# Last pass of a two-layer attention and MLP training step: weights turned from four neighbouring rows, sums in natural order, w2's gradient units moved out of w1's phase

## The chip, the cores and the metric

The kernel runs on one core of one Trainium2 chip. Its time is device microseconds of one execution. The kernel before took a median of 1111.3 us in 3 runs (1110.21 to 1113.48).

## The reference

The reference is the output and all gradients of two identical layers on two tokens (B = 2, one query position, D = 1024). The two layers share their weights, and each is attention over a cache and then an MLP:

```
def A(x): q = x @ wq; p = softmax(q . k_cache / sqrt(128)); o = p . v_cache; return o @ wo
          # 32 query heads, 4 cached heads of 16384 positions x 128, wq [1024, 4096], wo [4096, 1024]
def B(x): return gelu(layernorm(x) @ w1 + b1) @ w2 + b2        # w1 [1024, 3584], w2 [3584, 1024]
x = A_x
for layer in (0, 1):
    x = x + A(layernorm(x))
    x = x + B(layernorm(x))
out_0 = x
out_1..out_9 = gradients of x, k_cache, v_cache, wq, wo, w1, b1, w2, b2, by vjp with grad_out
```

All tensors are bfloat16. The gradients of the caches (out_2 and out_3) are 67 MB, those of the matrices 31 MB.

## The kernel before

The kernel makes four passes over the cache: attention forward for layer 0 and for layer 1 (`attn_fwd`), then backward for layer 1 and for layer 0 (`attn_bwd`). Each goes over 8 pairs of token and cached head, in 16 steps each, a step being 1024 cached positions; each 1 MB chunk of K or V serves four steps. Between the passes lie the MLP phases. The backward pass of layer 0 is the last pass, and it also forms and stores all the large gradients.

**The order of the work.** The program is first written down as a list of operations (`emit`), and each names the chunks (1 MB buffers) that it uses. `Program.run` then walks the list and issues on SP's queue the load of the next chunk as soon as a buffer fits it; an issued load waits, in that queue, until the earlier users of its buffer are done. `slots` at the end of the kernel says which piece of memory is a buffer of which kind, from which operation to which: "load" for inputs, "half" (512 KB) and "full" (1 MB) as staging for outputs. Sixteen tiles `slot_tiles` start as "load" buffers; three of them become "half" ones (`HALF_AT`, two of them just before w1's last phase) and four "full" ones (`FULL_AT`: steps 4, 8, 12, 16 of the last pass). Two more areas become staging later on (`marks["done", ...]`). `keep` lets a chunk of the same key stay in its buffer from one use to the next where there is room.

**A product with a turned weight.** The backward pass multiplies by transposed weights. In the last pass a chunk of four blocks of 128 weight rows is loaded by `ld_rows`, "(j p) n -> p j n": partition p gets rows p, 128 + p, 256 + p and 384 + p of the four. `turn_rows` (two instructions a chunk, line 433) transposes it on VectorE in blocks of 32 x 32 elements of 4 bytes, each a pair of bfloat16, into a second buffer; each block is written as 32 adjacent elements ("p (w j m)"). `turned_products` (line 483) then uses 128 x 128 pieces of it as TensorE weights against `vb`, a copy of the vector spread block-diagonally over four groups of 32 partitions by `spread` (lines 502 and 503). The sums come out in PSUM in an order that depends on the transpose: the quarter j of 32 rows of every group is in partitions 32 j to 32 j + 31, the group in the column. `unquad` brings them into natural order: one copy from PSUM to the tile `uq` (line 513) and 16 copies of 32 partitions each (lines 521 on VectorE, 523 on ScalarE, 525 on POOL, dealt out by its string `on`).

The chunks turned so in the last pass are

- w1, eight chunks of 896 columns (`ws1c`, turned by `t1`, multiplied by `p1`), before the pass, for the gradient of the MLP's input (`dm_0`, `mlp_in_bwd(0, ...)`);
- wo, two chunks for each of three cached heads (`wo_bwd_ops` through `turned_pair`), for the gradient of the heads' outputs, which `do_of` takes up;
- wq, two chunks for each of three cached heads (`wq_bwd_ops`), summed in PSUM and taken out once by `dn_kept` into `dnq`.

**w1's phase.** After the pass of layer 1: four transposes of w1 `t1[0:4]`, then the 28 products with w2 (`here_products`, line 461, sums `dhps0`) with `t1[4:9]` between them, then `dh0_` (line 1500) and its spread, then `t1[9:]`, and then the eight products `p1`. After each of these the kernel emits one or two pieces of `first`, the gradient of w2 (out_8): `y_rows` (line 1266) and `x_rows` (lines 1281 and 1286) build the two factors, each unit is one TensorE product of 512 columns (line 1303) and one eviction on ScalarE (line 272) or VectorE (line 275), and every fourth unit issues a store of 512 KB on POOL (line 1329). Nine pieces go between and behind the products, six after the sums of the layer norm (`g1p[0]`, line 645 on), the rest (`rest_h`) into the background list `bg`, from which the last pass takes `max(1.3, len(bg) / (120 - s))` pieces at each step s from 5 on. The sums end in `gA_all`, with which the last pass begins (`wo_prods0`).

**The end.** The last step is 133. The outputs of the caches are formed in units of 512 columns (line 1248); a chunk of 1 MB is stored by line 1253 after eight of them. The last pair's K chunks are worked off two steps at a time in steps 126 to 133, and what is left of the outputs, the last wq products and out_1 follow.

Of the kernel before, what the change touches and what calls it, by code (L numbers as in the profile page):

```python
# [10 lines left out]
I32 = mybir.dt.int32  # L11
# [10 lines left out]
SPARE = (3, 4)  # L22
HALF_AT = (-1, -1, 18)
FULL_AT = (4, 8, 12, 16)
N_HALF = len(HALF_AT)
N_FULL = len(FULL_AT)
SKEW = 2
# [151 lines left out]
def kernel(  # L179
# [98 lines left out]
    def dve(us):  # L278
        load_of("dve", us)
# [92 lines left out]
    def ld_rows(nm, W, j0, rb, c0, n):  # L372
# [2 lines left out]
            ap[:, 0:rb * n].rearrange("p (j n) -> p j n", j=rb),  # L375
            W[j0 * 128:(j0 + rb) * 128, c0:c0 + n].rearrange("(j p) n -> p j n", p=128)), (nm, j0, c0))

    def ld_wq(k):
        return [ld_rows("wq", A_wq, 4 * i, 4, k * 1024, 1024) for i in range(2)]

    def ld_wo(k):
        return [ld_rows("wo", A_wo, 8 * k + 4 * i, 4, 0, 1024) for i in range(2)]
# [41 lines left out]
            emit(*pend.pop(0))  # L424


    def turn_rows(c, t, ncol=1024):

        nw = ncol // 128

        def f(h):
            def fn():
                V.transpose(out=t.ap[:, h * nw * 256:(h + 1) * nw * 256].bitcast(I32).rearrange(  # L433
                    "p (w j m) -> p w j m", j=4, m=32), in_=c.ap[:, 0:4 * ncol].bitcast(I32).rearrange(
                        "p (j n) -> p j n", j=4)[:, :, h * nw * 32:(h + 1) * nw * 32].rearrange(
                            "p j (w m) -> p w j m", m=32))
                dve(1.23)
            return fn

        return [(f(h), [c, t]) for h in range(2)]  # L440
# [34 lines left out]
    def turned_products(ps, t, w0, nw, vb, first, last, parts=1):  # L475

        def f(k):
            def fn():
                tv = t.ap[:, 0:nw * 256].rearrange("p (w x e) -> p w x e", x=128, e=2)
                for w in range(k * nw // parts, (k + 1) * nw // parts):  # L480
                    for e in range(2):
                        J = (w0 + w) // 2
                        PE.matmul(ps(), lhsT=tv[:, w, :, e], rhs=vb()[:, 2 * (w % 2) + e, :, 2 * J:2 * J + 2],
                                  start=(first and w == 0 and e == 0), stop=(last and w == nw - 1 and e == 1),
                                  skip_group_check=True)
            return fn

        return [(f(k), [t]) for k in range(parts)]
# [17 lines left out]

        return (lambda: hold["vb"]), fn

    def unquad(dst, src, on="vag"):

        C = src.shape[1]
        q = small.tile([128, 8, 4, 2], F32, name="uq", bufs=1)[:, 0:C]
        V.tensor_copy(out=q, in_=src)
        n = 0
        for a in range(4):
            for j in range(4):
                d, s_ = dst[32 * a:32 * a + 32, :, j], q[32 * j:32 * j + 32, :, a]
                e = on[n % len(on)]
                n += 1
                if e == "v":  # L520
                    V.tensor_copy(out=d, in_=s_)
                elif e == "a":
                    S.copy(out=d, in_=s_)
                else:
                    GP.tensor_copy(out=d, in_=s_)
# [415 lines left out]
    def turned_pair(ws, acc, vb):  # L941

        ts = [P.chunk() for _ in ws]
        res = []
        for i in range(2):
            res += turn_rows(ws[i], ts[i]) + turned_products(lambda i=i: acc[:, i], ts[i], 0, 16, vb, False, True, 2)
        return res

    def wo_bwd_ops(l, k, vb):

        acc = sb[0][:, 64:80].rearrange("p (c a b) -> p c a b", c=2, a=4)

        def fin():
            raw = small.tile([128, 8, 2], F32, name="do_raw")
            unquad(raw[:].rearrange("p (c j) b -> p c j b", j=4), acc)
            V.memset(sb[0][:, 64:80], 0.0)
            dve(1.1)
            do_of(l, k, raw[:])

        return turned_pair(ld_wo(k), acc, vb), (fin, ())  # L960

    def wo_first_ops(l, k, ws=None):

# [35 lines left out]
    def wq_bwd_ops(l, k):  # L999

        acc = sb[0][:, 96:112].rearrange("p (c a b) -> p c a b", c=2, a=4)
        hold = {}

        def sp():
            vb, fn = spread(lambda: dq_all[:, k * R:(k + 1) * R, 2 * l:2 * l + 2], 8, "vg")
            hold["vb"] = vb
            fn()

        return [(sp, ())] + turned_pair(ld_wq(k), acc, lambda: hold["vb"]())

    def wq_last_ops(l, k):

# [7 lines left out]
    def attn_bwd(l, order, gT, wo_first, outputs=None, mark=None, extra=None):  # L1020
# [49 lines left out]
        dnq = wrk.tile([128, DJ, 2], F32, name="dnq")  # L1070

        def dn_kept():
            unquad(dnq[:].rearrange("p (c j) b -> p c j b", j=4),
                   sb[0][:, 96:112].rearrange("p (c a b) -> p c a b", c=2, a=4), "g")

        tail = []
        for i, k in enumerate(kvs):
# [313 lines left out]
    def at_sb0(c0, n):  # L1391
        return sb[0][:, c0:c0 + n]
# [79 lines left out]
    for n, b in enumerate(w2_turns):  # L1472
        extra.setdefault(28 + 3 * n, []).append(b)

    ws1c = [ld_rows("w1q", B_w1, 4 * h, 4, cg * 896, 896) for h in range(2) for cg in range(4)]
    dm_0 = quads(at_sb0(224, 16))
    vh0, spread_h0 = spread(lambda: dh_all[:, :, 0:2], FJ, "vh")
    t1, p1 = [], []
    for n, c in enumerate(ws1c):
        t = P.chunk()  # L1480
        t1 += turn_rows(c, t, 896)
        p1 += turned_products(lambda n=n: dm_0[:, n // 4], t, 14 * (n % 4), 14, vh0, n % 4 == 0, n % 4 == 3)
    for n, b in enumerate(t1[0:2]):
        extra.setdefault(135 + 2 * n, []).append(b)
# [24 lines left out]
        emit(*b)  # L1509
    emit(lambda: load_of("dve", 6.0))  # L1510
    first = [y_rows(gM_all, 0, 8, 0, 0)] + dw_units("h", 0, 0, pieces_rows(out_8, F, D))
    rest_h = first[15:]
    for n, b in enumerate(p1):
        emit(*b)
        for u in first[n + (n > 0):n + 2]:
            emit(*u)
    va0, spread_a0 = spread(lambda: gA_all[:, :, 0:2], DJ, "va")
    g1p = mlp_in_bwd(0, lambda dm: unquad(dm[:].rearrange("p (c j) b -> p c j b", j=4), dm_0), g2, parts=True)
    emit(g1p[0])
    emit(lambda: load_of("dve", 6.0))  # L1520
    for u in first[9:15]:
        emit(*u)
    emit(lambda: saved.__setitem__("g1", g1p[1]()))
    extra = {4: [(spread_a0, ())]}
# [22 lines left out]
    def outputs(s, rest=False):  # L1547
        if rest:
            fin = late.pop(s)
            return fin[0:1], sum([sched.pop(x) for x in sorted(sched)], []), bg + fin[1:]  # L1550
        if s in STAGE:
            mark(s)()
        if s in (68, 78):
            mark("done")(s // 78)
        res = list(sched.pop(s, ()))
        if s in late:
            bg.extend(late.pop(s))
        if s >= 5:
            state["credit"] += max(1.3, len(bg) / (120 - s)) if s < 116 else 3
        while bg and state["credit"] >= 1:  # L1560
            res.append(bg.pop(0))
            state["credit"] -= 1
        state["credit"] = min(state["credit"], 2.0)
        return res
# [2 lines left out]
    attn_bwd(0, down, lambda: saved["g1"], (va0, wo_prods0), outputs=outputs, extra=extra)  # L1567
    slots = []
    for i, t in enumerate(slot_tiles):
        until = marks[(HALF_AT + FULL_AT)[i], 0] if i < N_HALF + N_FULL else None  # L1570
        slots.append((t[:], "load", 0, until))
        if i < N_HALF:
            slots += [(t[:, j * 2048:(j + 1) * 2048], "half", until, None) for j in range(2)]
        elif i < N_HALF + N_FULL:
            slots.append((t[:], "full", until, None))
    slots += [(Et[1][:, i * CH:(i + 1) * CH], "load", 0, marks["e1", i]) for i in range(2)]
    slots += [(D1t[:, i * CH:(i + 1) * CH], "load", 0, marks["d1", 1 - i]) for i in range(2)]
# [37 lines left out]
```

## Time and profile before

| | |
|---|---|
| time, median of 3 runs | 1111.3 us (1110.21 to 1113.48) |
| time of the profiled execution | 1111.95 us |
| its span | 1110.2 us |
| TensorE, VectorE, ScalarE, POOL busy | 820.1, 762.1, 493.0, 182.5 us |
| mean granted TensorE clock | 0.722 |
| moved by DMA | 450.03 MB, mean 405 GB/s |
| loads (SP's queue), stores (POOL's queue) | 349.22 MB, 98.62 MB |

The span is the stretch between the first and the last record of the profile; the time includes 1.75 us around it. Busy times are sums over the whole span, through stages with different limits, so they don't say what bounds any of them. The mean rate is to be held against the rate in the slices where the DMA engines are full.

### The profile page before, as it was taken

To read this page: it belongs to the slowest core of one execution; us is meant where nothing else is said; L and a number is where in the kernel's file an instruction comes from. 1 tells how busy PE (TensorE), PEld (TensorE's weight loads), DVE (VectorE), ACT (ScalarE), POOL (GpSimd) and SP (SyncE) were. 2 spreads that over 40 slices of the span, in tenths; PEclk is the share of its full clock that TensorE was granted. 3 is DMA by queue.
4 is the path that set the end of the run, shared out by engine and by line. 5 is a ranking of instruction groups with operands and counts; after the bars stand their busy time and mean duration, and the time that the engine had idled before them with its cause. 6 is when DMAs were issued, how large, how long until landed. Compare 5 with 4: busy or idle time off the path is not lost. (4 is left out here: it accounts for less than half of the span.)

```text
span 1110.2 us, 34189 instructions
## 1 busy us (share of the span) xinstructions
PE 820.1 (74%) x14689; PEld 610.7 (55%) x14689; DVE 762.1 (69%) x1474; ACT 493.0 (44%) x1133; POOL 182.5 (16%) x577
## 2 busy tenths in 40 slices
PE   5665666457887647888778678978867986798886
PEld 4554565456777537887767564444433443344453
DVE  5864675069888637665646466978877895698874
ACT  0422223002233222245444327767766784577873
POOL 1000000001000000111111102324232332333331
PEclk9755555555555556568878658989997997699996
DMA  9999999999999998999999989999999999999994
GB/s 379 420 422 422 422 425 420 394 402 404 415 422 422 422 420 352 411 418 418 418 423 421 416 321 414 348 405 423 419 420 427 422 419 422 419 409 420 412 422 204
DMA packets 97448, 450.03 MB, mean 405 GB/s; under 512 B 7528, under 2 KB 11638, under 8 KB 58512
## 3 DMA queue, kind: packets, MB, share of 16 engines
q1 hardware_dynamic: 79504, 349.22, 77.2%
q0 software_dynamic: 17792, 98.62, 21.5%
q8 instruction: 115, 1.88, 0.6%
q14 instruction: 37, 0.30, 0.1%
HBM read 349.20 MB, written 98.62 MB: 403 GB/s over the span
## 5 line engine op out<-in xcount | busy, mean ns | idle before, releaser
L533 DVE STREAM_TRANSPOSE kT<-slot 128x512 int32<-128x512 int32 x420 | 283.4, 694 | 109.6 <-PE sc L546 86.6
L546 PE MATMUL sc<-qbd,kT 128*128 128x32 bf16 x4096 | 262.5, 222 | 11.9 <-DVE kT L533 10.4
L546 PEld LDWEIGHTS <-kT 128*128 128x128 bf16 x4096 | 209.2, 115 | 64.2 <-issue 33.3
L571 PEld LDWEIGHTS <-slot 128*128 128x128 bf16 x3520 | 144.5, 103 | 108.5 <-issue 48.1
L571 PE MATMUL sb<-xt,slot 128*128 128x8 bf16 x3520 | 161.2, 177 | 49.0 <-DMA slot<-in_A_v_cache_dram 24.4
L272 ACT CAST slot<-sc 128x512 bf16<-128x512 f32 x293 | 167.0, 593 | 64.4 <-PE sc L1303 38.9
L1248 PE MATMUL sc<-slot,late 128*128 128x512 bf16 x349 | 133.2, 404 | 17.4 <-DVE slot L275 5.4
L275 DVE CAST slot<-sc 128x512 bf16<-128x512 f32 x171 | 114.5, 678 | 30.6 <-PE sc L1248 16.2
L756 ACT ACTIVATE e<-sc 128x512 bf16<-128x512 f32 x32 | 19.0, 597 | 235.3 <-DVE sc L753 168.4
L272 ACT CAST slot<-sb 128x512 bf16<-128x512 f32 x139 | 82.5, 593 | 36.3 <-PE sb L1303 18.4
L451 ACT COPY slot<-tp 128x512 int32<-128x512 int32 x88 | 50.2, 586 | 108.6 <-PE tp L448 108.3
L448 PE MATMUL tp<-ident,slot 128*128 128x128 bf16 x768 | 72.0, 256 | 13.1 <-DMA slot<-in_A_wq_dram 7.1
L1248 PEld LDWEIGHTS <-late 128*128 128x128 bf16 x512 | 44.8, 99 | 59.5 <-issue 46.9
L581 ACT COPY xt<-e 32x128 int32<-32x128 int32 x256 | 75.6, 295 | 3.9
L1248 PE MATMUL sb<-slot,late 128*128 128x512 bf16 x163 | 66.6, 409 | 12.7 <-DVE slot L275 7.8
L1303 PE MATMUL sc<-slot,late 128*128 128x512 bf16 x160 | 64.4, 424 | 11.2 <-DVE e L275 6.2
L448 PEld LDWEIGHTS <-slot 128*128 128x128 bf16 x768 | 58.3, 117 | 15.7 <-DMA slot<-in_A_wq_dram 7.7
L433 DVE STREAM_TRANSPOSE slot<-slot 128x1024 int32<-128x1024 int32 (+1 forms) x48 | 55.3, 1178 | 16.0 <-DMA slot<-in_A_wo_dram 8.4
L275 DVE CAST slot<-sb 128x512 bf16<-128x512 f32 x81 | 54.9, 678 | 11.6 <-PE sb L1248 4.0
L638 POOL TENSOR_TENSOR m_rstd<-ln_vpe,neghalf 128x2 f32<-128x2 f32 x2 | 1.4, 716 | 349.8 <-DVE ln_vpe L636 349.8
L581 POOL COPY xt<-late 32x64 int32<-32x64 int32 x240 | 55.2, 230 | 13.0 <-DVE late L1042 1.9
L1253 POOL DMA_DIRECT2D out_dram<-slot x57 | 31.1, 546 | 157.1 <-ACT slot L272 115.2
(303 smaller groups left out, 1105.0 us busy)
## 6 DMA issues: line engine op xcount, KB each, us to landing
slot<-in_A_k_cache_dram SPq DMA_DIRECT2D x105, 1024.0 KB, 17.3
slot<-in_A_v_cache_dram SPq DMA_DIRECT2D x98, 1024.0 KB, 17.5
out_dram<-slot POOLq DMA_DIRECT2D x57, 1024.0 KB, 14.1
slot<-in_A_wq_dram SPq DMA_DIRECT2D x25, 1024.0 KB, 16.0
slot<-in_A_wo_dram SPq DMA_DIRECT2D x25, 1024.0 KB, 20.2
out_dram<-slot POOLq DMA_DIRECT2D x43, 512.0 KB, 14.2
slot<-in_B_w_dram SPq DMA_DIRECT2D x23, 896.0 KB, 15.5
slot<-in_B_w_dram SPq DMA_DIRECT2D x12, 1024.0 KB, 13.0
```

What stands on the lines that cost most here:

```text
L272: S.copy(out=dst, in_=src)
L275: V.tensor_copy(out=dst, in_=src)
L433: V.transpose(out=t.ap[:, h * nw * 256:(h + 1) * nw * 256].bitcast(I32).rearrange("p (w j m) -> p w j m", j=4, m=32), in_=c.ap[:, 0:4 * nc ...
L448: PE.transpose(tp[:, j * 128:(j + 1) * 128], c.ap[:, off + j * 128:off + (j + 1) * 128], ident[:])
L451: S.copy(out=d.bitcast(I32), in_=tp.bitcast(I32))
L533: V.transpose(out=kT[:].bitcast(I32).rearrange("p (w j m) -> p w j m", w=4, j=4), in_=c.ap[:, (i % 4) * 1024:(i % 4 + 1) * 1024].bitcast(I ...
L546: PE.matmul(sc[:, a0:a0 + 4, :, 2 * (i % 4) + q], lhsT=kv[:, 2 * q + w, :, e], rhs=qbd[:, q_at(g), 2 * w + e], start=(w == 0 and e == 0), ...
L571: PE.matmul(acc, lhsT=c.ap[:, n * 128:(n + 1) * 128], rhs=xv[:, i // 4, t // 2, :, 2 * (i % 4) + t % 2], start=(fresh and i == 0 and t == ...
L581: (GP.tensor_copy if on[t % len(on)] == "g" else S.copy)(out=d[32 * t:32 * t + 32, c0:c0 + cn, j, :], in_=s[32 * j:32 * j + 32, c0:c0 + cn ...
L1248: PE.matmul(ps, lhsT=hold["blk"][:, j, :], rhs=flat(qm(w)[:, (u % 2) * 4:(u % 2) * 4 + 4, :]), start=True, stop=True)
L1253: GP.dma_start((dKv if w == 0 else dVv)[g, :, c * 32:(c + 1) * 32, :], stg.ap.rearrange("p (t d) -> p t d", d=128))
L1303: PE.matmul(ps, lhsT=hold[j // 4 * 4][:, j % 4, :], rhs=Y.ap[:, y_at + c0:y_at + c0 + cn], start=True, stop=True)
```

## The change

- A new loader `ld_quads` reads "(p j) n -> p j n": partition p gets the four neighbouring rows 4 p to 4 p + 3. It takes the place of `ld_rows` for w1, wo and wq in the last pass (with keys of their own).
- `turn_rows` gets an order; for these chunks it is "w m j": each transposed element is written 4 elements, 16 bytes, from the one before. With both, the sums come out in natural order, partition by row and column by block.
- So `unquad` is not needed in `wo_bwd_ops` (`do_of` reads PSUM), in `dn_kept` (one VectorE copy) and in `mlp_in_bwd(0, ...)` (one VectorE copy). The uses of `unquad` that stay are those after the first pass of the MLP and in `mlp_in_bwd(1, ...)`; its default dealing goes from "vag" to "vgvagvvg".
- Of `first`, only `y_rows` and the first `x_rows` stay between the products of `p1` (after the fourth and the sixth); four units instead of six follow `g1p[0]`; nine more pieces go to the background list.
- Four more of the `slot_tiles` end as "load" buffers at steps 120, 122, 126 and 128 and become "full" ones (`TAIL_AT`).

```diff
+TAIL_AT = (120, 122, 126, 128)
...
+    def ld_quads(nm, W, j0, c0, n):
+        return P.chunk(lambda ap: nc.sync.dma_start(
+            ap[:, 0:4 * n].rearrange("p (j n) -> p j n", j=4),
+            W[j0 * 128:(j0 + 4) * 128, c0:c0 + n].rearrange("(p j) n -> p j n", j=4)), (nm, j0, c0))
...
-    def turn_rows(c, t, ncol=1024):
+    def turn_rows(c, t, ncol=1024, order="w j m"):
...
-                    "p (w j m) -> p w j m", j=4, m=32), in_=c.ap[:, 0:4 * ncol].bitcast(I32).rearrange(
+                    f"p ({order}) -> p w j m", j=4, m=32), in_=c.ap[:, 0:4 * ncol].bitcast(I32).rearrange(
...
-    def unquad(dst, src, on="vag"):
+    def unquad(dst, src, on="vgvagvvg"):
...
-            res += turn_rows(ws[i], ts[i]) + turned_products(lambda i=i: acc[:, i], ts[i], 0, 16, vb, False, True, 2)
+            res += turn_rows(ws[i], ts[i], order="w m j") + turned_products(lambda i=i: acc[:, i], ts[i], 0, 16, vb, False, True, 2)
...
         def fin():
-            raw = small.tile([128, 8, 2], F32, name="do_raw")
-            unquad(raw[:].rearrange("p (c j) b -> p c j b", j=4), acc)
+            do_of(l, k, acc.rearrange("p c a b -> p (c a) b"))
             V.memset(sb[0][:, 64:80], 0.0)
-            dve(1.1)
-            do_of(l, k, raw[:])
+            dve(0.1)
-        return turned_pair(ld_wo(k), acc, vb), (fin, ())
+        return turned_pair([ld_quads("woq", A_wo, 8 * k + 4 * i, 0, 1024) for i in range(2)], acc, vb), (fin, ())
...
-        return [(sp, ())] + turned_pair(ld_wq(k), acc, lambda: hold["vb"]())
+        return [(sp, ())] + turned_pair([ld_quads("wqq", A_wq, 4 * i, k * 1024, 1024) for i in range(2)], acc, lambda: hold["vb"]())
...
         def dn_kept():
-            unquad(dnq[:].rearrange("p (c j) b -> p c j b", j=4),
-                   sb[0][:, 96:112].rearrange("p (c a b) -> p c a b", c=2, a=4), "g")
+            V.tensor_copy(out=dnq[:], in_=sb[0][:, 96:112].rearrange("p (j b) -> p j b", b=2))
...
-    ws1c = [ld_rows("w1q", B_w1, 4 * h, 4, cg * 896, 896) for h in range(2) for cg in range(4)]
-    dm_0 = quads(at_sb0(224, 16))
+    ws1c = [ld_quads("w1q", B_w1, 4 * h, cg * 896, 896) for h in range(2) for cg in range(4)]
+    dm_0 = at_sb0(224, 16).rearrange("p (c a b) -> p c a b", a=4, b=2)
...
-        t1 += turn_rows(c, t, 896)
+        t1 += turn_rows(c, t, 896, "w m j")
...
-    rest_h = first[15:]
+    rest_h = first[6:]
     for n, b in enumerate(p1):
         emit(*b)
-        for u in first[n + (n > 0):n + 2]:
-            emit(*u)
+        if n in (3, 5):
+            emit(*first[n // 4])
...
-    g1p = mlp_in_bwd(0, lambda dm: unquad(dm[:].rearrange("p (c j) b -> p c j b", j=4), dm_0), g2, parts=True)
+    g1p = mlp_in_bwd(0, lambda dm: V.tensor_copy(out=dm[:], in_=dm_0.rearrange("p c a b -> p (c a) b")), g2, parts=True)
...
-    for u in first[9:15]:
+    for u in first[2:6]:
         emit(*u)
...
+        if s in TAIL_AT:
+            mark(s)()
...
-        until = marks[(HALF_AT + FULL_AT)[i], 0] if i < N_HALF + N_FULL else None
+        until = marks[(HALF_AT + FULL_AT + TAIL_AT)[i], 0] if i < N_HALF + N_FULL + len(TAIL_AT) else None
...
-        elif i < N_HALF + N_FULL:
+        elif until is not None:
             slots.append((t[:], "full", until, None))
```

## The prediction

> **What bounds the kernel now.** I read the page's slices first: the DMA engines are busy in almost all of them.
>
> ```profile
> DMA  9999999999999998999999989999999999999994
> GB/s 379 420 422 422 422 425 420 394 402 404 415 422 422 422 420 352 411 418 418 418 423 421 416 321 414 348 405 423 419 420 427 422 419 422 419 409 420 412 422 204
> ```
>
> At 420 GB/s the 450 MB need 1071 us of the 1110.2 us span. The change touches three of the places where the rate is lower or the end is decided, so I read windows there (columns: stretch, its length, busy time of each engine, granted TensorE clock, DMA share, GB/s).
>
> ```profile
> 645.00:655.00 10.00, 7.57 (x258) 7.30 (x258) 9.49 (x12) 1.90 (x1) 0.00 (x0) 0.50 0.91 312
> 655.00:670.00 15.00, 12.68 (x226) 8.85 (x225) 9.23 (x25) 7.90 (x18) 2.67 (x8) 0.50 0.81 304
> 670.00:695.00 25.00, 21.52 (x267) 12.63 (x266) 17.14 (x34) 17.79 (x38) 6.69 (x20) 0.86 1.02 420
> 695.00:730.00 35.00, 31.41 (x365) 16.90 (x364) 31.57 (x49) 27.62 (x51) 10.88 (x30) 1.00 0.93 349
> 730.00:1085.00 355.00, 290.93 (x3450) 155.57 (x3447) 280.28 (x480) 247.58 (x495) 118.14 (x349) 0.91 1.02 420
> 1085.00:1090.00 5.00, 4.13 (x49) 2.13 (x49) 2.61 (x6) 1.75 (x3) 0.53 (x1) 0.50 0.65 272
> 1090.00:1095.00 5.00, 5.00 (x77) 2.79 (x74) 1.75 (x3) 2.17 (x3) 0.53 (x1) 0.50 0.06 25
> ```
>
> So from 645 to 730 us the engines decide (loads wait for buffers: SP's queue waits once 23.0 us, to 701.06, for a kblock transpose), from 730 to 1085 the DMA decides, and after 1085 the engines again. A delay before 730 counts in full; a byte moved from before 730 to after it counts 1/420 us per KB; work between 730 and 1085 is covered by the transfers.
>
> The timeline of w1's phase (VectorE only) shows its chain:
>
> ```profile
> 645.15 7.22 DVE L433 STREAM_TRANSPOSE slot<-slot 128x896 int32<-128x896 int32 x7
> 652.29 0.18 DVE L1500 SCALAR_TENSOR_TENSOR dh_all<-sb,nslope 128x56 bf16<-128x56 f32 x1
> 653.92 7.52 DVE L433 STREAM_TRANSPOSE slot<-slot 128x896 int32<-128x896 int32 x7
> 664.54 0.17 DVE L513 COPY uq<-sb 128x16 f32<-128x16 f32 x1 [3.11 <-PE sb L483]
> 664.75 1.03 DVE L521 COPY dm_sb<-uq 32x4 f32<-32x4 f32 x6
> 666.69 0.17 DVE L645 TENSOR_TENSOR lb_t<-dm_sb,m_y 128x16 f32<-128x16 f32 x1 [0.91 <-ACT dm_sb L523]
> ```
>
> Already today the seven transposes end (652.37) when dhps0 is ready (TensorE's last product of w2 starts at 651.3); the second seven end at 661.44, 3 us before the products they feed (664.5).
>
> **1. The strided transposes.** All 40 transposes of the last pass (16 of w1, 12 of wo, 12 of wq) keep their size, but each int32 is now written 16 bytes from the one before instead of beside it. No long VectorE row of before writes so. The nearest by engine is the same instruction, written in runs; the nearest by pattern are TensorE's: L546 spreads 32 columns at least 32 bytes apart, L1229 writes 128 adjacent ones, L571 writes 8. From the groups by form between 740 and 1000 us:
>
> ```profile
> L433 DVE STREAM_TRANSPOSE slot<-slot 128x1024 int32<-128x1024 int32 x32 | 38.6, 1223 | 12.2 <-DMA slot<-in_A_wo_dram 8.4 <-DMA slot<-in_A_wq_dram 3.4 <-DMA slot<-in_B_w_dram 0.3
> ...
> L546 PE MATMUL sc<-qbd,kT 128*128 128x32 bf16 x608 | 32.3, 199 | 0.0
> L571 PE MATMUL sb<-xt,slot 128*128 128x8 bf16 x616 | 28.2, 176 | 0.0
> L1229 PE MATMUL tp<-ident,late 128*64 128x128 bf16 x80 | 8.9, 238 | 0.0
> ```
>
> (the first line is from the whole span). Spread: (199-176)/24 = 0.96 ns a column; adjacent: (238-176)/120 = 0.52. So the spread element costs about double. VectorE's own price is (1223-694)/512 = 1.03 ns an element (694 is L533's 512). The lower end is no change, since nothing gets shorter by writing farther apart; the upper, for which L546 is only a cousin, is three times. I take the double, by the pattern's row: +1.06 us for 1024 columns, +0.93 for 896.
>
> [...]
>
> On the path: seven transposes from 645.15 take 7.22 + 6.5 = 13.7 us and end at 658.9; the chain to the next seven takes what it does (652.37 to 653.92), 660.4; those take 7.52 + 6.5 = 14.0, to 674.4. The last product follows in 1.1 us (28 matmuls, 0.94 us, and a semaphore), the one copy in 0.2: L645 starts at 675.8 instead of 666.69. TensorE runs 0.8 us late behind two more units there today (gA_all written 669.37, wo's products 670.19); with four units instead of six I give back 0.6. **+8.5 us.** Were the price nothing, the same chain gains: w1's products without the five units and the x_rows between them (0.6 us each on TensorE) are left with 9.1 us of products, y_rows and one x_rows, and end 1.1 us sooner, unquad's 2.15 us become 0.2, and 0.6 as above: -3.7.
>
> The first wo pair of the pass runs at 714.96 to 730.55, with VectorE busy 31.57 of 35 us and the DMA not full: four transposes, +4.2, of which VectorE's gaps there take about 1.2. **+3.** The other 20 lie after 730: VectorE 280 of 355 us plus 21, hidden; a cover that fails would cost up to those 21.
>
> **2. The gradient units moved.** Eight units, an x_rows and two stores of 512 KB leave the phase (stores today at 662.35, 669.57, 671.53; one stays) for the queue worked off over steps 5 to 120, where nine more pieces on 115 steps are 0.08 a step. POOL issues the two stores later, 0.7 us each, in gaps. Their 1.05 MB leave a stretch where the DMA idles for one where it is full: **+2.5**.
>
> **3. The quads' loads.** wo's rows are whole, so four neighbours are 8 KB in one piece. The trace's records: a 2048-byte packet of a load takes 85.2 ns, one of 8192 bytes 313.3. A chunk of 1 MB: (512 x 85.2 - 128 x 313.3)/16 = 220 ns less. Six chunks, all in the full stretch: **-1.3**. wq and w1 are column strips, their pieces stay 2 KB and 1792 bytes: 0.
>
> **4. unquad elsewhere.** Three times for wo (738.28 to 740.87 the first), once for dnq on POOL (3.5 us at 1066): all in the full stretch, 0; uncovered the three would be worth 2.4 us each. The one that stays (L1458, 437.74) goes from six VectorE, five ScalarE, five POOL copies to eight, two, six; VectorE's two of 0.17 end it 0.2 later than POOL does now: **+0.2**.
>
> **5. Four more "full" buffers from step 120.** Only one eviction of the tail waits for a landing:
>
> ```profile
> 1063.01 0.57 POOL L1253 DMA_DIRECT2D out_dram<-slot  x1 [1.62 <-ACT ds L272]
> 1082.75 0.69 DVE L275 CAST slot<-sb 128x512 bf16<-128x512 f32 x1 [2.56 <-DMA out_dram<-slot]
> 1082.75 1.07 ACT L272 CAST slot<-sc 128x512 bf16<-128x512 f32 x2 [2.79 <-DMA out_dram<-slot]
> ```
>
> The store issued at 1063.01 landed 19.65 us later and held both evictors. With four buffers more the wait is gone; next comes TensorE, which is never idle from 1090 to 1095, and the DMA is empty there, so the whole **-2.7** reaches the end. The same four tiles stop holding loads: the last K load (issued 1057.17, 17.3 us to landing by the median) is read at 1085.85, 11 us of slack, so 0.
>
> Sum: 8.5 + 3 + 2.5 - 1.3 + 0.2 - 2.7 = +10.2 us. The profiled execution took 1111.95 us (span 1110.2); that makes 1122.2, and against the median of 1111.3, 0.65 lower, **1121.5 us**.
>
> **The rivals.** *Strided writes cost nothing* (VectorE writes one element a cycle wherever it lands). For it: L533, L433 and L469 all pay about 1.03 ns an element whatever they read. Against: the TensorE rows. Then -3.7 + 0 + 2.5 - 1.3 + 0.2 - 2.7 = -5.0: 1106 us, faster. The point that decides is the price of one transpose: at +0.4 us each (w1's phase 14 x 0.4, less some 3 us of slack and the 3.7) the change breaks even.
>
> *Strided writes cost three times*: another 13 us in w1's phase and 3 at 715: 1137, and VectorE (280 + 43 of 355) begins to bound the full stretch.
>
> *The tail's loads come too late*: the four tiles are closed to chunks used after their steps, and if the last K load slips by more than its 11 us, every further us is lost; with unchanged transposes and a slip of 17 us, 1112. Against: five tiles and an e slot remain for two wq and four K chunks.
>
> **How the numbers follow.** A measurement of this kernel tells 0.3% (3.3 us) from no change. Double price: 0.50, its own range 1114 to 1129; of it 0.02 faster, 0.03 same. Nothing: 0.33, 1102 to 1110; 0.29 faster, 0.03 same. Three times: 0.10, all slower. Late loads: 0.07; 0.01 faster, 0.02 same. Together 0.32 faster, 0.08 same, 0.60 slower. The range takes both likely cases, 1103 to 1128, leaving out the triple price and thin ends.
>
> **What would show it.** L433's 128x1024 form near 2.3 us where it is now 1.22 (right), or unchanged (then the rival, near 1106). L645 of the second mlp_in_bwd near 676 with the double price, near 663 without. Store L1329's first issue in w1's phase only after gA's sums. No eviction waiting on out_dram after 1040. If L433 is doubled and the time still falls, VectorE was not the chain of w1's phase; if it is unchanged and the time rises, the moved bytes or the tail's loads are at fault.

## The result and the profile after

The changed kernel takes a median of 1138.59 us (6 runs, 1136.55 to 1141.24) against 1112.95 us (6 runs, 1110.21 to 1114.44) for the kernel before: ratio 1.0235, 95% interval 1.0219 to 1.0252, slower by some 25.6 us. The forecast was 1121.5 us with a range of 1103 to 1128: the sign was right, the size was not. The profiled execution took 1138.39 us, its span is 1136.6 us, 26.4 us more than before's.

The page's slices of after (DMA share in tenths, GB/s):

```profile
DMA  9999999999999999999999958899989999999895
GB/s 378 421 421 423 422 424 418 392 392 404 419 421 424 419 419 345 421 414 420 419 422 420 377 224 362 322 413 421 408 335 417 424 421 422 423 421 423 323 421 222
```

Before had two dips in the second half (321 GB/s in w1's phase, 348 two slices on). After has that dip deeper (224), then 322 (around 710 us), 335 (around 830) and 323 (around 1060). Each is looked at below. The windows of after, at the same stretches as the prediction's (stretch, length, busy time of TensorE, its weight loads, VectorE, ScalarE, POOL, granted clock, DMA share, GB/s):

```profile
645.00:655.00 10.00, 6.16 (x225) 6.05 (x224) 9.68 (x13) 1.90 (x1) 0.00 (x0) 0.50 0.92 329
655.00:670.00 15.00, 7.68 (x212) 6.82 (x211) 14.43 (x10) 1.36 (x2) 0.00 (x0) 0.50 0.40 162
670.00:695.00 25.00, 19.34 (x232) 11.82 (x233) 14.46 (x36) 13.65 (x28) 2.59 (x4) 0.67 0.89 355
695.00:730.00 35.00, 28.61 (x277) 14.07 (x277) 27.42 (x43) 23.33 (x47) 10.83 (x32) 0.90 0.82 327
730.00:1085.00 355.00, 285.30 (x3319) 150.49 (x3319) 289.26 (x448) 237.60 (x460) 112.50 (x319) 0.92 0.99 402
```

From 655 to 670 VectorE is busy 14.43 of 15 us, in place of 9.23: it alone sets that stretch now. From 695 to 730 TensorE, VectorE and ScalarE each did less than before (VectorE 27.42 us against 31.57), which points at something that stopped them together. And from 730 to 1085, which the prediction called covered, the DMA moved 402 GB/s in place of 420.

To see where the 26.4 us lie I cut the spans at events that every version has: the layer norm's gradient at the end of the pass of layer 1 and the one after w1's phase (`lb_t`), and the starts of VectorE's products with `dl` at steps 10, 18, 26 and 106 of the last pass (us; e2, y4, y1 and z2 are experiments below).

| stretch | before | after | turns only (e2) | w1's turns only (y4) | move, mended (y1) | after, mended (z2) |
|---|---|---|---|---|---|---|
| w1's phase | 24.0 | 28.8 | 28.6 | 28.6 | 20.7 | 28.8 |
| to step 10 | 21.8 | 22.8 | 21.8 | 22.1 | 23.0 | 22.8 |
| step 10 to 26 | 44.9 | 52.8 | 49.8 | 47.2 | 44.8 | 46.8 |
| of it step 10 to 18 | 21.3 | 27.5 | 24.8 | 23.6 | 21.6 | 21.6 |
| of it step 18 to 26 | 23.6 | 25.3 | 25.0 | 23.6 | 23.2 | 25.2 |
| step 26 to 106 | 270.3 | 273.4 | 268.2 | 271.0 | 271.4 | 274.5 |
| step 106 to the end | 106.4 | 114.8 | 107.9 | 103.0 | 106.3 | 109.5 |

The part ahead of the change varies too: it ends at 642.73 us in the profile of before and between 643.7 and 647.6 in the others whose chunks come in one load, so single profiles carry 1 to 5 us there that are not the change's.

### The profile page after: what moved, and what is told of

The parts are those of the page before. It is cut to its first block, busy times and chain, and to the rows that moved or that the text cites. A ratio compares the mean times of both kernels' runs of the same rounds, so it can differ in the third digit from the quotient of the medians.

```text
span 1136.6 us, 34128 instructions
## 1 busy us (share of the span) xinstructions
PE 823.5 (72%) x14689; PEld 611.5 (54%) x14689; DVE 789.9 (69%) x1455; ACT 486.1 (43%) x1104; POOL 176.3 (16%) x542
## 5 line engine op out<-in xcount | busy, mean ns | idle before, releaser
L273 ACT CAST slot<-sc 128x512 bf16<-128x512 f32 x275 | 157.7, 592 | 71.8 <-PE sc L1307 28.5
L276 DVE CAST slot<-sc 128x512 bf16<-128x512 f32 x189 | 127.1, 679 | 46.5 <-PE sc L1252 24.4
L273 ACT CAST slot<-sb 128x512 bf16<-128x512 f32 x151 | 89.3, 591 | 48.9 <-PE sb L1307 20.4
L458 ACT COPY slot<-tp 128x512 int32<-128x512 int32 x88 | 50.1, 586 | 106.7 <-PE tp L455 106.4
L1252 PEld LDWEIGHTS <-late 128*128 128x128 bf16 x512 | 44.8, 99 | 77.8 <-issue 65.3
L440 DVE STREAM_TRANSPOSE slot<-slot 128x1024 int32<-128x1024 int32 (+1 forms) x48 | 82.7, 1764 | 4.6 <-DMA slot<-in_B_w_dram 4.3
L1252 PE MATMUL sb<-slot,late 128*128 128x512 bf16 x175 | 72.3, 413 | 14.5 <-ACT slot L273 6.0
L276 DVE CAST slot<-sb 128x512 bf16<-128x512 f32 x73 | 49.6, 680 | 13.2 <-PE sb L1252 8.4
## 6 DMA issues: line engine op xcount, KB each, us to landing
slot<-in_A_v_cache_dram SPq DMA_DIRECT2D x98, 1024.0 KB, 17.6
```

What stands on the lines that cost most here:

```text
L273: S.copy(out=dst, in_=src)
L276: V.tensor_copy(out=dst, in_=src)
L458: S.copy(out=d.bitcast(I32), in_=tp.bitcast(I32))
L1252: PE.matmul(ps, lhsT=hold["blk"][:, j, :], rhs=flat(qm(w)[:, (u % 2) * 4:(u % 2) * 4 + 4, :]), start=True, stop=True)
```

## The experiments

Times are medians, ratios are to runs of the kernel before on the same chip; square brackets hold 95% intervals. The median of before lay between 1112.12 and 1114.08 us from batch to batch, so a difference of medians of two batches carries up to 2 us. A loss given by a ratio is the ratio times 1113 us.

**One part at a time.** The four versions of the first batch take parts away from after or add one to before.

e1_adjacent, from after (the sums come out in another order):

```diff
-            res += turn_rows(ws[i], ts[i], order="w m j") + turned_products(
+            res += turn_rows(ws[i], ts[i], order="w j m") + turned_products(
...
-        t1 += turn_rows(c, t, 896, "w m j")
+        t1 += turn_rows(c, t, 896, "w j m")
```

> The changed kernel with one thing undone: the 40 transposes write their elements adjacent again (the sums then come out in another order, which leaves the results of out_1 and the gradients behind it in the wrong order; the work is the same). Theory S (strided writes are the whole loss): the transposes fall from 2.02 and 1.77 us to 1.22 and 1.05 us, and the time falls from 1138 to 1104-1110 us, at or under the kernel before. Theory T (the four tiles taken from the loads at steps 120 to 128 starve the end): the transposes fall, w1's phase gains its 5 us, and the time stays at 1122 or more. Theory M (the moved units and stores lengthen the last pass): likewise 1120 or more, lost evenly from step 5 on.

Measured 1128.03 us, 1.0131 [1.0105, 1.0157]. Without the stride w1's phase takes 19.9 us, 8.8 less than after and 4.0 less than before. The price of the stride is real, but 15 us of loss stay without it.

e2_turns_only, from after (new loads, strided turns, direct sums; w2's units stand between and behind `p1` as before):

```diff
-TAIL_AT = (120, 122, 126, 128)
+TAIL_AT = ()
...
-    rest_h = first[6:]
+    rest_h = first[15:]
```

> The changed kernel without the four tail buffers and without the moved units: only the new loads, the strided transposes and the direct sums. S: 1132-1142 us, as slow as the whole change or within 6 us of it. T or M: 1118-1126, since their part of the loss is gone.

Measured 1122.78 us, 1.0093 [1.0071, 1.0115]: the turns alone cost 10 us.

e3_tail_only, before with `TAIL_AT` alone:

> The kernel before with the four tail buffers alone. S: 1108-1112 us (the 2.7 us wait of the tail's evictions for a landing is gone, at most). T: 1118 or more, with the DMA rate falling under 350 GB/s in the last 80 us before the tail.

Measured 1113.42 us, 1.0005 [0.9991, 1.0019]: nothing, in place of -2.7.

e4_move_only, before with w2's units moved:

```diff
-    rest_h = first[15:]
+    rest_h = first[6:]
...
-        for u in first[n + (n > 0):n + 2]:
-            emit(*u)
+        if n in (3, 5):
+            emit(*first[n // 4])
...
-    for u in first[9:15]:
+    for u in first[2:6]:
```

> The kernel before with the units of w2's gradient moved alone. S: 1110-1116 us (1.1 and 0.6 us gained in w1's phase, 2.5 us lost to 1 MB that moves into the full stretch). M: 1120 or more.

Measured 1118.54 us, 1.0059 [1.0039, 1.0078]: +6.6 us by the ratio, 5.4 by the medians, although w1's phase gains 3.3 (20.7 us).

**Pairs.** The second batch: e5 (only the new loads and direct sums, adjacent writes), e6 (`TAIL_AT` and move on before), e7 (after without `TAIL_AT`), e8 (after without the move).

> Only the new loads and the direct sums, with adjacent writes, no tail buffers, units not moved (sums in another order, as in e1). Theory S (the strided write is what the turns cost, 10 us): 1104-1110 us, the gain of 2 us from unquad in w1's phase and 1.3 us from the 8 KB pieces and nothing lost. Theory Q (the loads of neighbouring rows or the direct sums cost by themselves, whatever the write): 1118-1124, as in e2.

> The kernel before with both the tail buffers and the moved units, no new turns. Additive (each part costs what it costs alone, 0 and 5.4 us): 1117-1120 us. Theory P (the two hinder each other: fewer buffers for loads while more units wait): 1126-1131, which would account for the 15 us that e1 loses without any strided write.

> The changed kernel without the tail buffers. Additive (9.7 + 5.4 us): 1126-1130 us. P: the same, as the pair is broken up. If turns and moved units hinder each other: 1135-1140, the whole loss of the change.

> The changed kernel with the units left in w1's phase. Additive (9.7 + 0 us): 1121-1125 us. P: the same. If turns and tail buffers hinder each other: 1130-1136.

| kernel | median us | ratio |
|---|---|---|
| e5_quads_adjacent | 1113.65 | 1.0005 [0.9989, 1.0021] |
| e6_tail_move | 1123.62 | 1.0088 [1.0059, 1.0118] |
| e7_turns_move | 1135.13 | 1.0187 [1.0154, 1.0221] |
| e8_turns_tail | 1130.44 | 1.0143 [1.011, 1.0177] |

e3, e4, e5 and e6 came out between the ranges written down for them. The new loads with direct sums are worth nothing by themselves, and e2, which differs from e5 by the stride alone, is 9.1 us slower by the medians. But e5's nothing is a balance: by its profile w1's phase is 2.0 us shorter than in before, and steps 10 to 18 are 3.9 us longer. The parts don't add: 10.4, 6.6 and 0.6 us alone by the ratios make 17.6, together it is 25.6. The tail buffers, harmless on before, cost 5.1 us more with the move (e6 against e4) and 7.7 more with the turns (e8 against e2) by the medians; by the ratios it is 3.2 and 5.6, and the intervals overlap. So I looked for what the move and the tail buffers each make wait.

**What the move makes wait.** VectorE's timeline of e4 and its windows at the dip:

```profile
694.17 0.69 DVE L275 CAST slot<-sb 128x512 bf16<-128x512 f32 x1 [0.27 <-issue]
698.70 0.69 DVE L275 CAST slot<-sc 128x512 bf16<-128x512 f32 x1 [3.84 <-DMA out_dram<-slot]
```

```profile
695.00:700.00 5.00, 1.22 (x4) 0.36 (x4) 1.30 (x2) 1.33 (x3) 0.74 (x1) 0.70 0.65 261
700.00:705.00 5.00, 5.00 (x43) 2.37 (x41) 2.93 (x7) 2.03 (x4) 0.57 (x1) 0.50 0.31 131
```

One eviction stands 3.84 us for the landing of a store and the engines nearly stop behind it (TensorE works 1.22 of 5 us). SP, which waits for their reads to end, issues no load from 675.50 to 705.65 (in y1 below it goes on at 701.03), and the DMA runs dry (131 GB/s). After has the same at 706.95:

```profile
706.95 0.69 DVE L276 CAST slot<-sc 128x512 bf16<-128x512 f32 x1 [4.15 <-DMA out_dram<-slot]
```

The profile of before has no such wait between steps 10 and 18 (those of e2, y4 and e5 have shorter ones, shown further down). Which buffer is it? First guess, the fourth full one, which comes at step 16 (x1_move_full14, e4 with `FULL_AT = (4, 8, 12, 14)`):

> The kernel before with the moved units, and the fourth full buffer given over at step 14 instead of 16. Theory F (the loss of the move is one wait: the chunk begun at step 14 must take the first full buffer, whose store lands late because the loads are issued in one burst; the evictions stand 3.8 us, no buffer is freed for SP, and the DMA runs dry for 5.3 us): the wait near 699 us is gone, the stretch from step 10 to 26 falls from 50.9 to about 45 us, and the time to 1110-1115. Theory B (the moved megabyte itself costs, in a stretch where the DMA is full): no change, 1117-1120.

Measured 1117.52 us, 1.0043 [1.0027, 1.0059]. The wait shrank to 2.86 us and stayed: not this one. Which operation takes which buffer follows from the program, and shows another. In e4 a half buffer's last use ends with the store issued at 689.61, and 23 operations later the next unit of w2's gradient takes it again, although a third tile is given up as half buffers only at step 18. In before at least 34 operations lie between. So y1_move_half12, e4 with that tile six steps earlier:

```diff
-HALF_AT = (-1, -1, 18)
+HALF_AT = (-1, -1, 12)
```

> Before with the moved units and the third half buffer tile given up at step 12 instead of 18 (two more 512 KB staging buffers six steps earlier). Theory H: the eviction that stands 3.84 us at 698.70 in the moved-units kernel (2.86 us with an earlier full buffer) waits for a half buffer whose store was issued 9 us before; with two more the wait is gone, step 10 to step 26 goes from 50.9 back to 45 to 46 us and the time from 1118.5 to 1113 to 1115. Rival F: the wait is that of a full buffer and of DMA that runs dry anyway: wait of 2 to 4 us stays near 698, time 1117 to 1119. Rival P: the pass pays for the moved megabyte wherever it lands: the wait is gone but the time stays within 1 us of 1118.5.

Measured 1112.27 us, 0.9994 [0.9982, 1.0006]. The windows of y1:

```profile
695.00:700.00 5.00, 4.92 (x53) 2.29 (x50) 4.28 (x8) 3.50 (x7) 1.75 (x4) 1.00 0.68 277
700.00:705.00 5.00, 4.46 (x51) 2.55 (x50) 4.44 (x8) 4.12 (x9) 1.27 (x2) 1.00 1.04 336
```

The engines go on (TensorE 4.92 us in place of 1.22), steps 10 to 26 take 44.8 us in place of 50.9, and the whole loss is gone. One staging tile that came too late was the price of the move. Of what w1's phase gains (3.3 us) little reaches the end all the same: by the table 1.2 us are given back by step 10 and 1.0 from step 26 to 106, where the DMA decides, and the ratio can't tell the rest from nothing.

**What the tail buffers make wait.** The chain of waits of after near the end (start, us, what; a DMA line is a transfer that the next line waited for):

```profile
1102.14 0.41 PE sb L578 x16
1102.58 9.65 DMA slot<-in_A_k_cache_dram
1112.23 0.05 issue
1112.28 0.58 PE sb L578 x16
```

The load of the last K chunk is issued when TensorE has read an earlier chunk to its end, at 1102.58 us, and TensorE stands 3.09 us for it. The SP queue of after and, in the second fence, of before:

```profile
1066.26 0.38 SPq L375 DMA_DIRECT2D slot<-in_A_wq_dram  x1
1083.02 0.33 SPq L370 DMA_DIRECT2D e<-in_A_k_cache_dram  x1
1102.58 0.33 SPq L370 DMA_DIRECT2D slot<-in_A_k_cache_dram  x1
```

```profile
1032.12 0.38 SPq L374 DMA_DIRECT2D slot<-in_A_wq_dram  x1
1057.17 0.33 SPq L369 DMA_DIRECT2D e<-in_A_k_cache_dram  x1
```

With four tiles closed to loads that outlive their steps, the first of the last two wq loads goes out at 1066.26 in place of 1032.12, the K loads stand behind it in the queue, and the last one finds no buffer until 1102.58. In e3 the same transfer is on the chain in place of the store that held before's evictors:

```profile
1078.37 9.40 DMA slot<-in_A_k_cache_dram
```

It costs e3 nothing net: TensorE waits 1.85 us for it where evictors waited 2.8. Counted from the kernel's own step 106, the last K load goes out after 53.4 us in before, 72.2 in e3, 78.4 in e6 and 80.8 in after, where the DMA is not full ahead of it (290 GB/s at 1060 to 1070). x5_move_tail2 closes only two tiles:

```diff
-TAIL_AT = (120, 122, 126, 128)
+TAIL_AT = (120, 122)
```

> The kernel before with the moved units and only two tail buffers (steps 120 and 122). Theory W (with four tiles closed to them the last two wq loads, which live to the end, wait at the head of SP's queue and hold up the K loads behind them): two more tiles for them take most of it away, 1117-1120 us, the stretch from step 106 to the end back from 112.4 to 105-108 us. Otherwise it stays at 1122-1126.

Measured 1119.42 us, 1.0063 [1.0046, 1.0079]: by the medians 4 us less than e6, as e4; the intervals of x5 and e6 overlap. The profiles are clearer: no K load is on the chain, and step 106 to the end is 106.3 us in place of e6's 112.4. The two late tiles were at fault. That expectation names the wq loads at the queue's head; the chain names the K load behind them, which the same closed tiles delay.

**The price of the stride.** x3_strides, after without `TAIL_AT`, gives each kind of chunk an order of its own:

```diff
-            res += turn_rows(ws[i], ts[i], order="w m j") + turned_products(
+            res += turn_rows(ws[i], ts[i], order=("w a m b", "j m w")[i]) + turned_products(
...
-        t1 += turn_rows(c, t, 896, "w m j")
+        t1 += turn_rows(c, t, 896, ("w m j", "w a m b", "m w j", "w j m")[n % 4])
```

> The changed kernel without tail buffers, whose transposes write with several spacings (the later sums then take wrong elements): w1's chunks in turn 16 bytes, 8 bytes, 112 bytes and adjacent; wo's and wq's first chunk 8 bytes, second 32 bytes. Theory L (what counts is how many elements fall into one 16-byte line): 8 bytes as adjacent, 1.05 us for 896 columns and 1.22 for 1024; 16, 32 and 112 bytes alike, 1.77 and 2.02. Theory D (the price grows with the distance): 8 bytes between, 112 bytes over 1.9 for 896.

One run, 1128.8 us. Its groups by form (mean ns is the number before the last bar; L444 writes every 16 bytes, L448 every 8, L451 every 112, L453 adjacent, L446 every 32):

```profile
L446 DVE STREAM_TRANSPOSE slot<-slot 128x1024 int32<-128x1024 int32 x12 | 24.2, 2017 | 0.0
L448 DVE STREAM_TRANSPOSE slot<-slot 128x1024 int32<-128x1024 int32 x10 | 12.2, 1220 | 0.0
L444 DVE STREAM_TRANSPOSE slot<-slot 128x896 int32<-128x896 int32 x4 | 7.0, 1777 | 4.3 <-DMA slot<-in_B_w_dram 4.3
L451 DVE STREAM_TRANSPOSE slot<-slot 128x896 int32<-128x896 int32 x4 | 7.0, 1811 | 0.1
L448 DVE STREAM_TRANSPOSE slot<-slot 128x896 int32<-128x896 int32 x4 | 4.2, 1092 | 0.0
L453 DVE STREAM_TRANSPOSE slot<-slot 128x896 int32<-128x896 int32 x4 | 4.2, 1079 | 0.0
```

At these spacings it is a step, not a slope: writes at every 8 bytes cost nearly what adjacent ones do (1.092 us for 1.079), at every 16 bytes 0.70 us more (1.777), and at every 112 bytes hardly more than that (1.811). For 1024 columns it is 0.80 us (2.017 at every 32 bytes for 1.220 at every 8). The times are those of theory L; that lines of 16 bytes lie behind them is not shown by them, and no spacing between 8 and 16 bytes was run.

**Where the stride costs.** y4_w1_strided, e2 with wo, wq and their `unquad` as before:

> Only w1 turned from four neighbouring rows with 16-byte spaced writes and its sums direct; wo, wq and their unquads as before; no tail buffers, no move. Theory S (each strided transpose costs where it stands): w1's phase 28.6 us, +4.7, last pass as before: 1117 to 1118; the other 5 us of the kernel with all three (1122.8) then are wo's and wq's. Rival: the late start of the last pass makes all of it: 1121 to 1123. Rival: w1's phase is paid back by the pass and wo and wq make the loss: 1113 to 1115.

Measured 1119.17 us, 1.0068 [1.0046, 1.009], between two of the ranges written down. w1's turns make 7.6 of the 10.4 us by the ratios, 4.7 of it in w1's phase by the profile. Adding wo's and wq's (e2) lengthens steps 10 to 26 from 47.2 to 49.8 us, and all from step 26 on from 374.1 to 376.1.

Not all of this is the price of transposes. VectorE's timelines of e2, y4 and e5 each have a wait for a store's landing between steps 10 and 18 (one line each, in this order):

```profile
704.75 1.29 DVE L276 CAST slot<-sc 128x512 bf16<-128x512 f32 x2 [2.70 <-DMA out_dram<-slot]
703.64 1.29 DVE L276 CAST slot<-sc 128x512 bf16<-128x512 f32 x2 [1.41 <-DMA out_dram<-slot]
697.41 1.29 DVE L276 CAST slot<-sc 128x512 bf16<-128x512 f32 x2 [1.75 <-DMA out_dram<-slot]
```

Steps 10 to 18 take 24.8, 23.6 and 25.2 us there, against 21.3 in before. Steps 18 to 26, which hold the first wo pair's four transposes, take 25.0 us in e2 and 23.6 in y4 and e5. So by single profiles some 4.7 of e2's 10 us are w1's phase, 3.5 the stretch with the wait and 1.5 the first wo pair. e5 has the wait without any strided write. Which buffer it is stays open; in z1 and z2 below, with the third tile's half buffers at step 12, it is gone and steps 10 to 18 take 21.6 us. e2 with that tile at step 12 was not run.

**Natural order without the stride.** If a chunk is loaded so that group q of 32 partitions holds rows 128 q + 32 j + m, adjacent writes give natural sums. x2_natural_loads does it with four loads of 32 partitions a chunk (with the move and x1's full buffer, without `TAIL_AT`), y2_wide_natural with four loads of 128 partitions a chunk, one for each j (without move and `TAIL_AT`), y3_wide_move_half12 is y2 with the move and y1's half buffer.

```diff
+            for q in range(4):
+                nc.sync.dma_start(
+                    ap[32 * q:32 * q + 32, 0:4 * n].rearrange("m (j n) -> m j n", j=4),
+                    W[(j0 + q) * 128:(j0 + q + 1) * 128, c0:c0 + n].rearrange("(j m) n -> m j n", j=4))
```

in x2, and in y2 and y3

```diff
+            rows = W[j0 * 128:(j0 + 4) * 128, c0:c0 + n].rearrange("(q j m) n -> j q m n", q=4, j=4)
+            for j in range(4):
+                nc.sync.dma_start(ap[:, j * n:(j + 1) * n], rows[j])
```

> The changed kernel with the natural order made by the load instead of by the write: partition m of quarter q gets rows 128 q + 32 j + m (four loads of 32 partitions a chunk), the transposes write adjacent, so the sums are in natural order and unquad stays out; units moved; no tail buffers; fourth full buffer at step 14. If the stride, the tail buffers and the wait at step 14 are the whole loss: 1105-1112 us, w1's phase 4 us shorter than before. If four small loads a chunk or the direct sums cost: 1118 or more.

> Only the natural order of the sums, without strides: each chunk of w1, wo and wq in the last pass comes in four loads, one for each quarter j, each over all 128 partitions (partition 32 q + m gets row 128 q + 32 j + m), transposes write adjacent elements, sums are read directly; no tail buffers, no move. Theory: the 128-partition loads cost as the one load of before, w1's phase is 22.0 us as with four neighbouring rows and adjacent writes, time 1111 to 1114 (ratio 1.000). Rival: loads in four parts cost as the four loads of 32 partitions did (205 to 254 GB/s before w1's phase): above 1120.

> The wide natural loads of the kernel before this one, with the moved units and the third half buffer tile at step 12. If theory H holds and the loads cost nothing: w1's phase 20 us (4 less than before), step 10 to 26 at 45 to 47, time 1108 to 1111. If the last pass takes back whatever w1's phase gives: 1112 to 1114. If the move's wait stays: 1117 to 1119.

Measured: x2 1140.21 us, 1.0252 [1.0233, 1.0272]; y2 1257.97 us, 1.1308 [1.1287, 1.1328]; y3 1255.47 us, 1.1284 [1.1266, 1.1301]. My theory failed for all three. The windows of x2 and then of y2 while w1's chunks come in:

```profile
640.00:660.00 20.00, 8.45 (x279) 8.14 (x280) 8.06 (x19) 0.00 (x0) 0.52 (x1) 0.50 0.92 205
660.00:680.00 20.00, 10.79 (x321) 9.90 (x318) 12.47 (x17) 3.26 (x3) 0.00 (x0) 0.50 1.03 254
```

```profile
660.00:680.00 20.00, 0.00 (x0) 0.00 (x0) 4.21 (x4) 0.00 (x0) 0.00 (x0) 0.50 0.26 101
```

In x2 the DMA share is 0.92 and 1.03, and about half of the 420 GB/s is moved (205 and 254); in y2 the share is 0.26, and a quarter is moved (101). Before moves 350 and 345 GB/s from 640 to 660 and from 660 to 680 us, at shares of 0.94 and 0.88.

**Both causes mended in the kernel after.** z1_after_half12 is after with `HALF_AT = (-1, -1, 12)`, z2_after_half12_tail2 has `TAIL_AT = (120, 122)` as well.

> The kernel after with the third half buffer tile at step 12 instead of 18, nothing else. Theory: the moved units' price is that one wait in this kernel too; the eviction that stands 4.15 us at 706.95 goes on at once, and the time falls by the 5.3 us that the stage was dry for and what follows it, to 1129 to 1133. Rival: in this kernel the move costs by what it loads on a DMA queue that the strided turns leave full, and giving a load buffer up at step 12 changes nothing: 1136 to 1139.

> The kernel after with the third half buffer tile at step 12 and with only the first two of the four tail buffers (steps 120 and 122). Theory: both waits gone, only the strided turns' price is left: 1122 to 1126, as the kernel with the turns alone (1122.8). Rival: the three parts cost more together whatever the buffers: 1129 and up.

Measured z1 1132.0 us, 1.0177 [1.0153, 1.0202], and z2 1129.68 us, 1.015 [1.0125, 1.0175]. The half buffer is worth 6.6 us here too, and steps 10 to 26 take 46.8 us in place of 52.8. The two tail tiles: the K load leaves the chain and step 106 to the end goes from 116.1 us (z1) to 109.5 in the profiles, but the medians differ by 2.3 us with intervals that overlap (z1's profiled execution, 1134.85 us, is the slowest of its four). z2's rival was the nearer one: by the medians 6.9 us more than e2 remain. z2 still closes two tiles to the tail's loads; turns, move and the earlier half buffers without any tail buffer were not run.

## Why the prediction was wrong, point by point

The chain of w1's phase was forecast rightly, at 3.7 us too much; the steps that failed lie behind it. Term 2 priced the moved units by their bytes (+2.5) and put the wait for a staging buffer at nothing: that wait is worth 6.6 us. Term 5 held the last K load's slack against a load that would not move: it slipped by 27 us even against the kernel's own step 106. And the cover after 730, taken as whole for each part, let through some 7 us when the parts came together; the mechanism of that stays open. The time, 1138.6 us, is near the 1137 of the rival with three times the price; that is chance, as the transposes cost 1.6 times what they did before.

**Term 1, the price of a strided transpose: the step was right in kind, its size too high.** I took double, +0.93 and +1.06 us, from TensorE's spread columns. The trace has +0.69 (L440's 896 form, 1773 ns against 1087) and, in x3, +0.80. w1's phase in after:

```profile
646.43 11.84 DVE L440 STREAM_TRANSPOSE slot<-slot 128x896 int32<-128x896 int32 x7
658.12 0.20 DVE L1504 SCALAR_TENSOR_TENSOR dh_all<-sb,nslope 128x56 bf16<-128x56 f32 x1
659.76 12.19 DVE L440 STREAM_TRANSPOSE slot<-slot 128x896 int32<-128x896 int32 x7
672.59 0.17 DVE L1522 COPY dm_sb<-sb 128x16 f32<-128x16 f32 x1 [0.63 <-PE sb L490]
672.79 0.17 DVE L652 TENSOR_TENSOR lb_t<-dm_sb,m_y 128x16 f32<-128x16 f32 x1
```

The chain is the forecast one, transposes, slope, transposes, one copy, L652, with the 1.5 us behind the slope that before has too and 0.63 us of waiting for TensorE; only the seven take 11.84 and 12.19 us in place of 13.7 and 14.0. The phase grew by 4.8 us, not 8.5. The branch without a price was forecast at -3.7 and measured at -4.0 (e1). L652 at 672.79 lies between the two marks of my list (676 and 663), 3 us from the first. The break-even that I gave, +0.4 us a transpose, doesn't follow from its bracket, which is -1.1 us there (14 x 0.4 less 3 and 3.7); with the same terms it is near +0.5. The measured price lies above either.

**The first wo pair, +3: mis-sized, +1.5 to +2.1.** From y4 to e2 steps 10 to 26 grow by 2.7 us, which looks like the forecast, but only 1.5 of it lies in steps 18 to 26, where the pair is turned (2.1 from y1 to z2); the rest goes with the longer wait for a landing ahead of it.

**"The other 20 lie after 730, hidden": true alone, false in company.** From step 26 to the end before takes 376.8 us, e2 376.1 (with all strided turns), y1 377.7 (with the moved units), z2, with both, 384.0. The stretch hides either load but not the two together: 7.2 us more than before, 7.9 more than e2. z2's two tail tiles are part of that company, but not all of it: e7, which has no tail buffers, takes 381.0 us. I had checked the cover against VectorE's mean (280 of 355 us), and each part separately. The DMA's rate from 730 to 1000 (before, e2, after, one fence each; e2 and after are 12 and 15 us later in their work, and from step 26 to 106 the rates are 420, 416 and 411 GB/s):

```profile
730.00:1000.00 270.00, 218.93 (x2537) 115.02 (x2535) 209.56 (x364) 183.41 (x365) 88.04 (x259) 0.89 1.02 420
```

```profile
730.00:1000.00 270.00, 223.63 (x2605) 118.44 (x2608) 223.34 (x350) 182.78 (x352) 84.33 (x243) 0.91 1.01 413
```

```profile
730.00:1000.00 270.00, 217.35 (x2554) 114.98 (x2554) 221.84 (x346) 180.53 (x349) 82.56 (x236) 0.92 0.99 406
```

VectorE's mean went only from 209.6 to 221.8 of 270 us, but ScalarE's evictions now stand for landings (17.8 us in six waits of over 0.4 us in after), for example

```profile
815.01 0.59 ACT L273 CAST slot<-sc 128x512 bf16<-128x512 f32 x1 [4.92 <-DMA out_dram<-slot]
```

just ahead of the slice with 335 GB/s. Between 720 and 1050 ScalarE and VectorE together have 16.4 us of such waits in e2 and 30.9 in e5, without the loss, so these waits by themselves don't explain it; y1 and y4, with wo's and wq's old loads and sums, have at most 2.7 us. Which of the waits turns into a dry DMA when both loads are there was not settled, nor whether it takes the stride: e1, which has the new loads and sums, the move and the tail buffers but no strided write, is 4.4 us slower than e6, which has the last two alone (medians; the intervals overlap).

**Term 2, the move, +2.5: mis-sized, +6.6.** I counted its bytes against the full stretch and POOL's time for the stores, not the staging buffers that the moved units take. One half buffer came back too early; with two more in time the term is 0 (y1, 0.9994), so the 2.5 us for the bytes were not there either.

**Term 5, tail buffers, -2.7 with slots at 0: failed.** The wait at 1082.75 is gone as forecast. But I held 11 us of slack against an unmoved last K load, and that load slipped 45 us, from 1057.17 to 1102.58 (27 of it against the kernel's own step 106). It was the rival "the tail's loads come too late", at 0.07; the buffers that I counted against it ("five tiles and an e slot remain for two wq and four K chunks") did not suffice. By the profiles the stretch from step 106 to the end is some 6 us longer for it (e6 against x5, z1 against z2); the medians show 4.2 and 2.3, with intervals that overlap.

**Terms 3 and 4, -1.3 and +0.2:** not told apart; e5, which has them and the direct sums, is at 1.0005 [0.9989, 1.0021], with the gain and the wait named above in it. Of my list, no eviction waits more than 0.5 us for out_dram after 1040 in after, as written.

Undone one after the other, by the medians: the half buffer is 6.6 us of the 25.5 (after to z1), the tail's last K load 2.3 (to z2, within the intervals of nothing), what the parts cost only together 6.9 (to e2, with the caveats above), the turns 9.7 (to before in e2's batch, 1113.11). In another order the shares would differ, as e2 has a wait for a landing of its own that z1 and z2 have lost. That my +10.2 is near the turns' 9.7 is luck: w1's phase was 3.7 us too high and the first wo pair about 1, and that unforeseen wait made up for most of it. The move stood in my sum with +2.5, the tail buffers with -2.7, their loss in company with nothing.

## What to carry to other kernels

Moving output work costs the staging buffers that it takes at its new place: list which buffer each moved unit gets and how long ago its last store was issued; here six steps earlier for one tile was worth 6.6 us. A buffer taken from the loads is paid by the last chunk that no longer finds one (here its load went out 45 us later), so write the load plan to its end instead of arguing from slack in the old one. Two edits that each hide in a stretch can fail to hide together (here 7.2 us from step 26 to the end): check the cover against their sum.

## What the runs showed of the hardware that I had not expected

- The price of VectorE's spaced writes was a step between the spacings of 8 and 16 bytes (x3, 896 columns: 1.079 us adjacent, 1.092 at every 8 bytes, 1.777 at every 16), nearly flat from there to 112 bytes (1.811); the order that writes pairs together cost 0.01 us more than adjacent writes.
- With each chunk's load in four parts less was moved while w1's chunks came in. With four loads of 32 partitions (x2) it was 205 GB/s from 640 to 660 us and 254 from 660 to 680, at a DMA share of 0.92 and 1.03; before has 350 and 345 at 0.94 and 0.88. With four loads over 128 partitions whose source is four blocks of 32 rows (y2) it was 101 from 660 to 680, at a share of 0.26. What slowed either was not shown.
- The mean granted TensorE clock was 0.722 in the profile of before and 0.910 in that of y1, whose times are 1111.95 and 1112.65 us: between these two the clock did not show in the time.
